# Output tiles in the spent v weights, and a new hand-written order, in a fused attention and GELU kernel

## The chip, the cores and the metric

The kernel runs on one core of one Trainium2 chip. The time is the device time of one execution in microseconds; the figure that is compared is the median over the runs. Before the change it is 206.4 us (three runs, 206.39 to 206.58). Beside the timed runs there is one profiled execution with a trace. Its own time is 207.25 us, and its span, from the first to the last instruction, is 205.3 us. Engines are named as the profile names them: PE (matmul), PEld (weight load), DVE (vector), ACT (scalar), POOL, and SP, which issues most of the DMAs.

## The reference

For x of 2048 rows by 640 columns in bf16, the result is x + A + B, where both branches start from one layer norm of x:

```python
xn = _layernorm(x, axis=-1)
return x + _A_ref(xn, A_wqkv, A_wo) + _B_ref(xn, B_w1, B_b1, B_w2, B_b2)
```

A is local attention with 32 heads of 20 columns. Every row attends to 8 rows, itself and those 2, 4, ... 14 rows back; rows before the start are masked. Queries, keys and values are xn @ wqkv, and the result goes through wo. B is a dense layer of 1536 columns with a bias and a tanh GELU, and a second dense layer with w2 and a bias.

## The kernel before

The rows are cut into 4 chunks of 512, each of 4 blocks of 128. Chunk n and block j or bl are the digits in the names of pieces below. Every piece is a short function that emits a few instructions, and the list ORDER (lines 42 to 74) gives the order in which all pieces are emitted. No scheduler moves anything afterwards: each engine runs its own instructions in the order of the list and waits, at an instruction, for the semaphores of what it needs. A piece that stands early in the list can therefore hold back everything behind it on its engine.

For one chunk the work is this.

- Statistics (`st` on DVE, or `su`, `ng`, `sq` on ACT for chunks 2 and 3), `rs` (square root on ACT, which loads a table), `rc` (reciprocal on DVE), and `xn`, the normalised rows (DVE in chunk 0, ACT after that).
- Transposes. Chunk 0 uses PE (`tp`) and copies out of PSUM (`tc`). Chunks 1 to 3 use one DMA transpose per block on SP's queue (also named `tc`, line 295). Chunk 1's stand at tc10 to tc13.
- Projections into q, k and v, transposed. In chunk 0 they are made in halves of 256 columns: `ga`, `gb`, `gd`, `ge` for q of the first pair of blocks, then `hj` followed by type (0 q, 1 k, 2 v), pair and column group, with the casts `hc` on ACT (line 398). Later chunks use `pj` (five 128x512 matmuls, line 339) and `pc` (a cast on ACT, line 403).
- Scores: eight `qk` products on DVE (line 436), then sums that fold five tiles into fewer, `pa` (line 471), in the buffer `half`. PE then adds the heads in `lg` (line 479) and ACT copies the logits (`cl`). The softmax follows on DVE and ACT (`mask`, `m`, `mx`, `ex`, `ss`, `ri`, `at`), and SP spreads the weights over partitions (`xd`, line 554).
- Values: eight `av` products on DVE (line 563), one sum `aa` that is an accumulating DMA on POOL's queue (line 573) in chunks 0 to 2 and a DVE instruction in chunk 3, then `ab` and `ot` on DVE. `half` is used again for the next chunk.
- The dense branch: `f1` (five matmuls, line 595) into PSUM and `ge` (GELU on ACT, line 611). The hidden tiles of chunk 3 lie in the spent q and k weights.
- The output: `o` followed by chunk, block and part 0 to 4. Parts 0 to 3 multiply hidden tiles with w2, part 4 multiplies `ot`'s result with wo (lines 631 and 633). `oc` copies the sum to a bf16 tile `osb` on ACT, and `od` adds it to the rows of the result by an accumulating DMA on POOL's queue. The last block goes another way (`oclo`, `ohi`, `ochi`, `ochd`).
- The result's rows are first written with x (`xp0`, `xp1`, `xp2`, on SP's queue) and then get the bias b2 (`xb`, on POOL's queue). `ldx`, `ld2` and `ldo` load the rest of x, then w2, then wo with b2.

Two pools matter for the order. `psA` has 6 PSUM buffers for nearly all results of PE but `o`; a matmul group waits until ACT has emptied an older buffer. `outp` has 2 tiles `osb`, so that an `oc` waits until the `od` before the last has landed.

The order before puts the weights' loads and the row copies among chunk 1's transposes on SP's queue: tc13, xp0, tc10, tc11, tc12, xp2, ldo, ld2.

Of the kernel before, what the change touches and what calls it, by code (L numbers as in the profile page):

```python
# [41 lines left out]
ORDER = """
wb st00a sum1 wa pad01 st00 rs00 ldx rc00 xn00a tp00a xn00b tp00b tc00a ga neg1 sq1 rs01 rc01 tc00b gb2 mean1 xn01
tp01 gb3 gb4 tc01a gd tc01b ho ge gc1 st03a st03 rs03 gc0 hj102 rc03 hc102 tb b1 hj101 hc101 st02a st02 rs02 hj100
hc100 xn03 tp03 tc03 pk hj202 rc02 xn02 tp02 tc02 gc4 hj201 hc201 hj111 st11a st10a hc111 st12a hj012 hc012 st11 hc202
st13a st13 hj112 hc112 st10 st12 rs1 qk010 rc1 qk000 qk011 hj110 f10_0 ge0_0 hj212 xn13 qk001 xn10 tc13 xn11 hc212
pa010 hj011 hj010 hc010 f10_11 f10_2 hc110 hc011 qk031 qk021 ge0_11 f10_10 xp0 qk020 pa000 su23 f10_6 xn12 ge0_10
qk030 pa020 su21 tc10 tc11 su22 hj200 hc200 f10_3 ge0_3 pa030 pa011 f10_9 tc12 su20 ng2 sq21 ge0_9 pa021 pj101 pc101
ge0_2 sq23 pj111 pj102 pj114 pc114 xp2 pc102 pj110 pc110 pj104 pa001 ge0_6 pa031 lg0 pc111 cl0 ldo xb3 xb2 pc104 mask
m0 mx0 ex0 pj112 pj103 pc103 pj113 pc113 ss0 ri0 pad11 pj100 pc100 pc112 qk121 qk120 hj211 sq20 hc211 qk101 ld2 pj124  # L50
qk100 sq22 pc124 f10_4 rs2 f11_6 pj121 rc2 ge0_4 pa120 qk110 f11_2 f10_1 ge0_1 pa121 qk111 xn21 pj123 pc123 ge1_6
pa122 pa100 pa110 xn23 f10_7 ge0_7 f11_8 tc23 f11_0 o000 xn20 tc20 tc21 ge1_2 f10_5 ge1_0 xb0 xn22 tc22 qk131 at0 xd00
ge1_8 f11_3 ge1_3 pa111 qk130 su32 pa101 pc121 f10_8 ge0_8 pad02 hj210 f11_5 pa130 pj120 pc120 pj200 pc200 pa112 pj211
pc211 pj210 pj212 pa131 pa102 pc210 hc210 pad12 pa132 lg1 av000 cl1 pj202 ge0_5 pj214 pc202 pj204 av001 aa00 m1 xd02
av021 pad21 av020 xd01 av011 av010 pj220 pj203 su33 ge1_5 su31 su30 ng3 sq33 xd03 av031 o001 pc212 pc203 o002 pc214
sq30 ab00 ot00 aa02 aa01 sq32 sq31 pj213 pc213 xp1 pj221 pj224 rs3 av030 ab02 pj122 pc122 pad22 rc3 ot02 o003 o004
oc00 od00 pj201 mx1 ex1 ss1 ri1 at1 xn31 pc220 xn30 f11_9 o020 o021 o022 o023 xd10 ab01 ot01 pc204 o024 oc02 pc201
aa03 tc30 ab03 f11_4 pc224 o030 o031 o032 pj223 o033 ot03 o034 xn33 av100 f12_3 av101 aa10 xn32 pc223 xd12 av120 xd13
f12_0 f11_11 av130 oc03 pc221 o010 o011 ge2_3 f12_11 o012 ge2_11 ge1_4 ge1_9 xd11 av110 av111 aa11 o013 o014 av121
pj222 pc222 av131 aa13 tc31 tc33 tc32 pj302 pj322 pj300 pc322 pj314 pc314 pj312 ab10 f11_1 ge1_11 ge1_1 f11_7 pj303  # L60
qk201 ot10 qk200 pa200 pc312 ge2_0 pj301 pc301 ab11 pa201 f11_10 pc302 ge1_10 qk211 ot11 od02 qk210 ab13 qk231 ot13
pj324 pc324 pj304 pc304 pa210 qk230 aa12 qk221 ab12 ge1_7 pj311 pa211 oc01 ot12 pa230 od01 f13_2 qk220 pc311 f12_8
pa212 od03 ge3_2 pa220 pc300 o130 pa231 pj313 pa221 o131 o132 o133 o134 oc13 pj310 f13_0 pc303 pc310 ge2_8 xb1 o120
pa202 pa232 pa222 lg2 o121 o122 pad31 pc313 qk300 f13_6 qk311 cl2 m2 qk310 f13_10 qk331 mx2 ge3_6 f13_8 qk330 ge3_0
f13_3 ge3_3 pa310 o123 qk301 o124 ex2 ss2 oc12 od12 f12_7 qk320 ri2 pa311 at2 xd23 pa330 pa300 qk321 f12_4 o110 o111
o112 pa301 o113 ge3_10 f12_10 pa320 pa312 o114 oc11 ge2_10 f12_6 f13_7 ge3_7 ge3_8 ge2_7 o100 o101 pa321 f12_2 xd21
od13 pa331 pa302 pa322 f12_5 o102 o103 ge2_6 ge2_5 o104 pa332 lg3 od11 oc10 od10 pj323 av210 pc323 av211 f12_9 cl3 m3
f13_1 xd22 xd20 ge3_1 pj321 av230 f12_1 ge2_1 aa21 av231 f13_5 ge3_5 av201 av200 aa23 f13_9 mx3 ge2_2 ge2_4 aa20 ab21
f13_4 ge2_9 ot21 ex3 ss3 ri3 ge3_4 f13_11 ge3_11 av220 ab23 o210 o211 at3 xd30 o212 o213 o214 ot23 oc21 od21 av221
aa22 pj320 o330 ab20 pc321 ot20 ge3_9 pad32 pc320 av300 o310 av301 o200 o201 o202 o203 o204 oc20 od20 o311 o230 o231  # L70
xd31 av310 o232 xd32 o233 o234 oc23 o312 o220 o221 o222 av311 aa31 ab22 ot22 o223 o224 od23 oc22 od22 av321 o313 av320
aa32 ab32 ot32 o320 o321 o322 o323 o324 oc32 od32 ab31 ot31 o314 oc31 od31 o300 xd33 o301 o302 o303 aa30 av331 ab30
ot30 o304 oc30 od30 av330 aa33 ab33 ot33 o331 o332 o333 o334 ohi xl oclo ochi ochd
""".split()


# [720 lines left out]
```

## Time and profile before

| what | value |
|---|---|
| median of 3 runs | 206.4 us |
| profiled execution: own time | 207.25 us |
| profiled execution: span | 205.3 us |
| PE busy | 200.1 us, 97% |
| DVE busy | 181.6 us, 88% |
| ACT busy | 127.1 us, 62% |
| POOL busy | 34.6 us, 17% |
| granted TensorE clock | 1.00 in every stretch |
| DMA moved | 31.77 MB, mean 155 GB/s |

The chain of waits that ended last goes through PE for 90% of the span. Busy times overlap between engines, and one matmul's row is longer than the distance to the next matmul on PE: the rows of 128x512 matmuls are 379 ns long, while five of them, started one behind the other, take 1.08 us. So this document counts PE's work by the distance between starts: 0.216 us for 512 columns, 0.109 us for 256 and 0.056 us for 128. ACT's and DVE's instructions overlap by some 0.1 us as well, and sums over a queue use distances between starts there too: 0.48 us for a cast of 512 columns, 0.27 us for 256, 0.58 us for a GELU, 0.81 us for an `xn`, 1.40 us for a `qk` or an `av`, 1.14 us for the first `pa` of a block and 0.60 us for its others.

### The profile page before, as it was taken

Reading aid. Unit: us, or ns where it says so; the run is one execution under the profiler, and the core shown is the slowest. Engines: PE = TensorE matmul, PEld = TensorE weight load, DVE = VectorE, ACT = ScalarE, POOL = GpSimd, SP = SyncE. Lnnn points to the kernel's source line nnn. Section 1 sums busy time; section 2 is a strip of 40 time slices with the busy share of each in tenths; the row PEclk is TensorE's granted clock in tenths of the full one; section 3 lists DMA queues with packets and bytes.
Section 4 is the critical chain, followed back from the end, with each engine's and each line's share of the span. In section 5 each row is a group of like instructions: output and inputs, shape, how many; then the busy total and the mean of one; then the engine's idle time right before and its main releaser. Section 6 shows DMA issues by size and latency. Waiting matters only on the chain.

```text
span 205.3 us, 3230 instructions
## 1 busy us (share of the span) xinstructions
PE 200.1 (97%) x1261; PEld 111.1 (54%) x1261; DVE 181.6 (88%) x226; ACT 127.1 (62%) x246; POOL 34.6 (17%) x49
## 2 busy tenths in 40 slices
PE   8899999999999999999999999999999999999994
PEld 3798655464454555554555555445544455555552
DVE  3489999389998999769999999899998999699992
ACT  6388998999966998856425735564535794111210
POOL 2000000440000242202260060003104223111120
PEclk9999999999999999999999999999999999999999
DMA  6999599899259299989999067005462997972253
GB/s 209 390 395 374 185 140 323 303 258 199 58 100 252 86 173 190 156 128 182 189 188 191 8 73 122 0 0 68 103 134 32 164 190 118 209 116 28 28 66 64
DMA packets 27335, 31.77 MB, mean 155 GB/s; under 512 B 9272, under 2 KB 22072, under 8 KB 27320
## 3 DMA queue, kind: packets, MB, share of 16 engines
q0 software_dynamic: 7408, 12.78, 39.0%
q1 hardware_dynamic: 19600, 18.58, 32.8%
q8 instruction: 10, 0.16, 0.3%
q10 hardware_dynamic: 312, 0.20, 0.3%
q14 instruction: 5, 0.04, 0.1%
HBM read 10.00 MB, written 7.54 MB: 85 GB/s over the span
## 4 chain that ended last, share of the span: by engine, by line
PE 90%; DMA 4%; ACT 3%; issue 1%; SPq 0%; DVE 0%
PE lo L631 29%; PE pps L339 24%; PE hps L595 22%; PE hi L633 7%; PE gps L383 5%; DMA wq_sb<-in_A_wqkv_dram 3%; DMA xnT<-xn 2%; ACT xn L266 2%; PE gps L352 1%; PE L L479 1%; ACT qT L398 1%; PE tp L283 0%; ACT trash L224 0%; ACT hT L611 0%; SPq L131 0%
## 5 line engine op out<-in xcount | busy, mean ns | idle before, releaser
L595 PE MATMUL hps<-xnT,w_sb 128*128 128x512 bf16 x240 | 55.6, 379 | 0.0
L436 DVE TENSOR_TENSOR half<-qT,kT 128x2560 bf16<-128x2560 bf16 x32 | 46.7, 1484 | 1.0 <-PE L L479 0.9
L631 PE MATMUL lo<-w_sb,hT 128*128 128x512 bf16 x144 | 41.3, 379 | 0.0
L595 PEld LDWEIGHTS <-w_sb 128*128 128x128 bf16 x240 | 23.1, 98 | 26.2
L471 DVE TENSOR_TENSOR half<-half 128x1024 bf16<-128x1024 bf16 (+1 forms) x44 | 36.5, 881 | 0.0
L638 ACT CAST osb<-lo 128x512 bf16<-128x512 f32 x15 | 8.8, 584 | 37.1 <-PE hi L633 18.3
L633 PE MATMUL hi<-w_sb,hT 128*128 128x128 bf16 x144 | 31.5, 219 | 0.0
L611 ACT ACTIVATE hT<-hps,b1T 128x512 bf16<-128x512 f32 x36 | 24.0, 692 | 6.5 <-PE hps L595 5.6
L563 DVE TENSOR_TENSOR half<-vT,x_sb 128x2560 bf16<-128x2560 bf16 x16 | 23.0, 1487 | 3.3 <-DMA x_sb<-e 3.2
L644 POOL DMA_DIRECT2D out_dram<-osb x15 | 13.7, 959 | 72.2 <-ACT osb L639 72.2
L573 POOL DMA_DIRECT2D half<-half x12 | 15.6, 1302 | 56.0 <-DVE half L563 56.0
L563 DVE TENSOR_TENSOR half<-vT,ax 128x2560 bf16<-128x2560 bf16 x16 | 23.0, 1482 | 1.2 <-PE L L479 1.2
L631 PEld LDWEIGHTS <-hT 128*128 128x128 bf16 x144 | 14.1, 98 | 17.2 <-issue 0.4
L631 PE MATMUL lo<-wo,oT 128*128 128x512 bf16 x80 | 23.1, 379 | 0.0
L339 PE MATMUL pps<-xnT,wq_sb 128*128 128x512 bf16 x75 | 18.5, 380 | 0.4 <-DMA xnT<-xn 0.4
L339 PE MATMUL pps<-xnT,wv_sb 128*128 128x512 bf16 x75 | 18.3, 379 | 0.0
L339 PE MATMUL pps<-xnT,wk_sb 128*128 128x512 bf16 x75 | 18.0, 379 | 0.0
L633 PE MATMUL hi<-wo,oT 128*128 128x128 bf16 x80 | 16.9, 219 | 0.0
L176 ACT ACT_TABLE_LOAD x12 | 15.4, 1283 | 0.9 <-PEq L781 0.7
L633 PEld LDWEIGHTS <-hT 128*128 128x128 bf16 x144 | 14.1, 98 | 1.9
L582 DVE TENSOR_TENSOR half<-half 128x1280 bf16<-128x1280 bf16 x16 | 13.1, 821 | 0.5 <-DMA half<-half 0.4
L403 ACT CAST vT<-pps 128x512 bf16<-128x512 f32 x15 | 8.8, 587 | 6.9 <-PE pps L339 6.9
(91 smaller groups left out, 262.3 us busy)
## 6 DMA issues: line engine op xcount, KB each, us to landing
half<-half POOLq DMA_DIRECT2D x12, 640.0 KB, 6.9
w_sb<-in_B_w_dram SPq DMA_DIRECT2D x4, 960.0 KB, 11.3
out_dram<-osb POOLq DMA_DIRECT2D x15, 160.0 KB, 3.5
ax<-e SPq DMA_DIRECT2D x8, 256.0 KB, 4.7
x_sb<-e SPq DMA_DIRECT2D x8, 256.0 KB, 4.9
out_dram<-b2bc POOLq DMA_DIRECT2D x3, 640.0 KB, 9.6
x_sb<-in_A_x_dram SPq DMA_DIRECT2D x1, 1280.0 KB, 12.9
out_dram<-x_sb SPq DMA_DIRECT2D x2, 640.0 KB, 4.7
```

Source lines behind the costliest of these rows:

```text
L176: nc.scalar.activation(warm[:], nc.const_aps.tensor(0.0, [P, 1], F32), func)
L339: nc.tensor.matmul(ps[:], lhsT=wqkv_p[which][:, ti, to, :], rhs=xnT[:, ti, :], start=(ti == 0), stop=(ti == KT - 1),)
L436: nc.vector.tensor_tensor(out=half[:, j, h], in0=q[:, :, at].unsqueeze(1).to_broadcast([P, W // 2, KT, P]), in1=window(k, h, at), op=ALU.mult,
L471: nc.vector.tensor_tensor(out=kept, in0=kept, in1=gone, op=ALU.add)
L563: nc.vector.tensor_tensor(out=half[:, j, h], in0=window(qkv_tile(n, 2), h, cs), in1=ax_view(n)[:, j, ws, :].unsqueeze(2).to_broadcast([P, ...
L573: nc.gpsimd.dma_start(a, b, accum_op=ALU.add, max_dma_last_dim=CUT)
L582: nc.vector.tensor_tensor(out=a, in0=a, in1=b, op=ALU.add)
L595: nc.tensor.matmul(ps[:], lhsT=w1_sb[:, ti, ft * P : (ft + 1) * P], rhs=tiles["xnT", n][:, ti, :], start=(ti == 0), stop=(ti == KT - 1),)
L611: nc.scalar.activation(hT, tiles["hps", n, ft][:], ACT.Gelu_apprx_tanh, bias=b1T[:, ft : ft + 1], scale=1.0)
L631: nc.tensor.matmul(lo[:], lhsT=lhs, rhs=rhs[:, 0:CH], start=first, stop=last)
L633: nc.tensor.matmul(hi[:, 0 : D - CH], lhsT=lhs, rhs=rhs[:, CH:D], start=first, stop=last)
L644: nc.gpsimd.dma_start(rows, tiles["osb", n, bl][:], accum_op=ALU.add)
```

## The change

The tiles `osb` of chunk 3 and of block 0 of chunk 2 no longer come from the pool `outp`. They lie in the weights of v, which hold five slots of 128x640:

```diff
+    def out_tile(n, bl):
+        if (n, bl) == (2, 0) or n == NCH - 1:
+            return wqkv[2][:, bl if n == NCH - 1 else BPC, :]
+        return outp.tile([P, D], BF16, tag="osb", name="osb")
+
     def do_oc(n, bl):
-        osb = outp.tile([P, D], BF16, tag="osb", name="osb")
+        osb = out_tile(n, bl)
 ...
     def do_oclo():
-        osb = outp.tile([P, D], BF16, tag="osb", name="osb")
+        osb = out_tile(*last)
```

The list ORDER is new throughout; it holds the same pieces. Its part up to chunk 1's `lg`:

```diff
-wb st00a sum1 wa pad01 st00 rs00 ldx rc00 xn00a tp00a xn00b tp00b tc00a ga neg1 sq1 rs01 rc01 tc00b gb2 mean1 xn01
-tp01 gb3 gb4 tc01a gd tc01b ho ge gc1 st03a st03 rs03 gc0 hj102 rc03 hc102 tb b1 hj101 hc101 st02a st02 rs02 hj100
-hc100 xn03 tp03 tc03 pk hj202 rc02 xn02 tp02 tc02 gc4 hj201 hc201 hj111 st11a st10a hc111 st12a hj012 hc012 st11 hc202
-st13a st13 hj112 hc112 st10 st12 rs1 qk010 rc1 qk000 qk011 hj110 f10_0 ge0_0 hj212 xn13 qk001 xn10 tc13 xn11 hc212
-pa010 hj011 hj010 hc010 f10_11 f10_2 hc110 hc011 qk031 qk021 ge0_11 f10_10 xp0 qk020 pa000 su23 f10_6 xn12 ge0_10
-qk030 pa020 su21 tc10 tc11 su22 hj200 hc200 f10_3 ge0_3 pa030 pa011 f10_9 tc12 su20 ng2 sq21 ge0_9 pa021 pj101 pc101
-ge0_2 sq23 pj111 pj102 pj114 pc114 xp2 pc102 pj110 pc110 pj104 pa001 ge0_6 pa031 lg0 pc111 cl0 ldo xb3 xb2 pc104 mask
-m0 mx0 ex0 pj112 pj103 pc103 pj113 pc113 ss0 ri0 pad11 pj100 pc100 pc112 qk121 qk120 hj211 sq20 hc211 qk101 ld2 pj124
 ...
+ho sum1 pad02 st00a tb st00 wb rs00 neg1 sq1 rc00 xn00a tp00a xn00b tp00b ldx mean1 tc00a rs01 rc01 pad01 xn01 tp01
+tc01a tc00b tc01b b1 st03a ga gb2 gb3 gb4 gd ge gc1 hj101 st03 rs03 gc4 st02a st02 gc0 rc03 xn03 rs02 rc02 hj100 tp03
+tc03 xn02 tp02 tc02 st11a st11 hj201 hc100 hj102 hc102 hc101 hj212 hc212 hj011 hc011 hc201 hj112 hc112 st10a st10
+st13a st13 st12a st12 wa rs1 f10_0 ge0_0 qk011 hj111 hc111 rc1 xn12 tc12 qk001 xn10 tc10 hj012 qk000 qk010 hj010 xn11
+hj110 hc110 pa000 hc012 pk hc010 qk020 qk021 su22 qk030 qk031 tc11 xn13 tc13 ld2 f10_3 pa020 pa001 ldo xp0 xb0 f10_9
+hj200 ge0_9 hj202 hc202 pa021 f10_11 ge0_11 pa010 f10_8 su21 su20 su23 ng2 f10_2 ge0_3 hc200 sq20 ge0_2 xp2 pj102
+pc102 pj110 sq21 pc110 pj101 pc101 ge0_8 pa030 pa011 pj111 pj100 pc100 pj112 pa031 pc111 lg0 cl0 pj104 xb2 pc112 mask
+m0 mx0 ex0 ss0 pad11 pj113 pj103 pc103 ri0 pc104 pj114 pc114 pc113 qk130 qk100 qk131 qk121 pj123 pc123 sq23 f11_5 sq22
 ...
```

On SP's queue chunk 1's transposes now come first, in the order tc12, tc10, tc11, tc13, and behind them stand ld2, ldo, xp0 and xp2. The end of the list:

```diff
-aa22 pj320 o330 ab20 pc321 ot20 ge3_9 pad32 pc320 av300 o310 av301 o200 o201 o202 o203 o204 oc20 od20 o311 o230 o231
-xd31 av310 o232 xd32 o233 o234 oc23 o312 o220 o221 o222 av311 aa31 ab22 ot22 o223 o224 od23 oc22 od22 av321 o313 av320
-aa32 ab32 ot32 o320 o321 o322 o323 o324 oc32 od32 ab31 ot31 o314 oc31 od31 o300 xd33 o301 o302 o303 aa30 av331 ab30
-ot30 o304 oc30 od30 av330 aa33 ab33 ot33 o331 o332 o333 o334 ohi xl oclo ochi ochd
+ot20 f13_11 pad32 pc321 av311 av310 xd33 o310 o330 xd32 o200 o201 o202 o203 o204 ge3_8 oc20 ot23 o311 aa31 ab31 o230
+o231 xb3 av330 o232 o233 o234 oc23 av331 o312 ab22 ot22 o220 o221 o222 o223 o224 av320 ge3_11 o313 av321 aa32 ab32
+ot32 ot31 oc22 od22 o320 o321 o322 o323 xd30 o324 av300 av301 aa30 ab30 ot30 oc32 o314 oc31 od31 od23 o300 o301 o302
+aa33 od20 o303 o304 oc30 od32 ab33 od30 o331 o332 ot33 o333 o334 xl oclo ohi ochi ochd
```

The stores od31, od23, od20 and od32 now stand together near the end of POOL's queue, and xb3, which stood with xb2, stands behind od21. Every engine has the same matmuls, vector operations, activations, table loads and DMAs as before, in another order.

More of the change, by code (lines that the diff above doesn't have):

```diff
@@ L48 @@
-qk030 pa020 su21 tc10 tc11 su22 hj200 hc200 f10_3 ge0_3 pa030 pa011 f10_9 tc12 su20 ng2 sq21 ge0_9 pa021 pj101 pc101
-ge0_2 sq23 pj111 pj102 pj114 pc114 xp2 pc102 pj110 pc110 pj104 pa001 ge0_6 pa031 lg0 pc111 cl0 ldo xb3 xb2 pc104 mask
-m0 mx0 ex0 pj112 pj103 pc103 pj113 pc113 ss0 ri0 pad11 pj100 pc100 pc112 qk121 qk120 hj211 sq20 hc211 qk101 ld2 pj124
-qk100 sq22 pc124 f10_4 rs2 f11_6 pj121 rc2 ge0_4 pa120 qk110 f11_2 f10_1 ge0_1 pa121 qk111 xn21 pj123 pc123 ge1_6
-pa122 pa100 pa110 xn23 f10_7 ge0_7 f11_8 tc23 f11_0 o000 xn20 tc20 tc21 ge1_2 f10_5 ge1_0 xb0 xn22 tc22 qk131 at0 xd00
@@ L53 @@
[L53 to L67, printed above, removed]
@@ L68 @@
-f13_1 xd22 xd20 ge3_1 pj321 av230 f12_1 ge2_1 aa21 av231 f13_5 ge3_5 av201 av200 aa23 f13_9 mx3 ge2_2 ge2_4 aa20 ab21
-f13_4 ge2_9 ot21 ex3 ss3 ri3 ge3_4 f13_11 ge3_11 av220 ab23 o210 o211 at3 xd30 o212 o213 o214 ot23 oc21 od21 av221
-aa22 pj320 o330 ab20 pc321 ot20 ge3_9 pad32 pc320 av300 o310 av301 o200 o201 o202 o203 o204 oc20 od20 o311 o230 o231
-xd31 av310 o232 xd32 o233 o234 oc23 o312 o220 o221 o222 av311 aa31 ab22 ot22 o223 o224 od23 oc22 od22 av321 o313 av320
-aa32 ab32 ot32 o320 o321 o322 o323 o324 oc32 od32 ab31 ot31 o314 oc31 od31 o300 xd33 o301 o302 o303 aa30 av331 ab30
@@ new lines @@
+hj110 hc110 pa000 hc012 pk hc010 qk020 qk021 su22 qk030 qk031 tc11 xn13 tc13 ld2 f10_3 pa020 pa001 ldo xp0 xb0 f10_9
+hj200 ge0_9 hj202 hc202 pa021 f10_11 ge0_11 pa010 f10_8 su21 su20 su23 ng2 f10_2 ge0_3 hc200 sq20 ge0_2 xp2 pj102
+pc102 pj110 sq21 pc110 pj101 pc101 ge0_8 pa030 pa011 pj111 pj100 pc100 pj112 pa031 pc111 lg0 cl0 pj104 xb2 pc112 mask
+m0 mx0 ex0 ss0 pad11 pj113 pj103 pc103 ri0 pc104 pj114 pc114 pc113 qk130 qk100 qk131 qk121 pj123 pc123 sq23 f11_5 sq22
+rs2 rc2 f10_5 hj211 hc211 qk120 qk101 pa130 f10_4 ge0_4 xn22 tc22 ge0_5 qk111 hj210 hc210 pj121 xn20 at0 pa120 pj124
@@ new lines @@
+pc124 f11_2 xn23 f11_0 qk110 f11_8 ge1_8 tc23 f11_3 pa100 tc20 ge1_5 f10_7 ge0_7 pa121 xn21 f10_1 ge0_1 f10_10 ge1_3
+pa101 pa110 pc121 o000 ge1_0 f10_6 ge0_6 f11_6 pj120 pa102 pc120 su30 tc21 ge1_6 pj213 pj202 pc202 pad12 pa131 pa111
+pa122 xd00 pa112 pj211 pa132 lg1 ge0_10 o001 pj210 pc213 pc211 xd03 av001 pj200 pc200 cl1 pc210 ge1_2 av000 pj201
+pc201 xd02 av020 pj220 aa00 av021 aa02 m1 mx1 pj214 pc214 av030 av031 pj203 su31 su32 su33 xd01 ab00 pj122 ot00 ng3
+sq30 av010 f11_10 xp1 av011 pc122 ab02 ex1 ot02 o002 ss1 ri1 f11_4 aa03 ab03 pj212 pc212 o003 o004 oc00 od00 sq33
@@ new lines @@
+pc203 ot03 sq31 sq32 rs3 f12_11 at1 xd10 pj224 pc224 pad21 xd13 pad22 xd12 aa01 xd11 o020 o021 o022 o023 o024 oc02 rc3
+xn32 xn31 tc31 tc32 ab01 ot01 pj222 pc222 o030 o031 o032 xn30 tc30 pc220 o033 o034 oc03 pj204 pc204 o010 o011 av101
+av100 av120 aa10 av131 av110 av111 aa11 av121 f11_11 ge1_11 av130 aa13 xn33 tc33 f12_0 ge1_4 f11_1 ge1_1 qk201 ge2_0
+o012 o013 o014 f11_7 f13_2 ge1_7 pj223 pc223 ab10 ot10 qk200 pa200 f11_9 ge1_9 f12_3 ge2_3 od03 ge2_11 ab11 qk211
+pj324 pc324 pj313 pc313 pj302 ot11 qk210 ab13 pj310 pc310 oc01 ot13 qk230 aa12 f12_7 qk231 pj311 pc311 pj314 pc314
@@ new lines @@
+ab12 ge2_7 pj303 pc303 o130 pa230 o131 pj312 o132 ge1_10 pa210 pa201 pc312 f13_10 pa231 od02 ot12 pad31 pj301 qk221
+o133 qk220 o134 oc13 pa211 pa212 pj300 pc302 pc300 pc301 o120 pj304 ge3_2 pc304 o121 f13_4 pa220 ge3_10 pa202 pa221
+ge3_4 pa232 pa222 lg2 cl2 qk300 m2 mx2 qk330 qk331 qk301 o122 qk311 ex2 ss2 ri2 qk310 o123 f12_8 ge2_8 pa300 f12_2 at2
+xd20 xd22 f12_5 pa301 pa330 xd23 pa310 f12_4 f13_3 ge3_3 od01 ge2_4 xd21 o124 oc12 xb1 od12 f12_6 pa331 o110 pa311
+od13 o111 o112 o113 f13_6 ge3_6 qk320 o114 oc11 f13_9 o100 o101 qk321 o102 pa320 ge2_2 ge3_9 pa312 f13_7 ge3_7 ge2_5
@@ new lines @@
+pj322 pc322 f12_1 ge2_1 pj221 pc221 o103 o104 oc10 pa321 od11 pa302 pa322 pa332 lg3 av210 av211 pj320 pc320 pj323
+f13_0 ge3_0 f12_10 ge2_10 av230 av231 od10 cl3 ge2_6 av200 m3 f12_9 mx3 ex3 ge2_9 av201 f13_1 ge3_1 o210 aa21 ab21
+f13_8 ot21 ss3 av221 aa23 ri3 aa20 at3 xd31 pj321 f13_5 ge3_5 av220 aa22 o211 o212 ab23 o213 o214 pc323 ab20 oc21 od21
+ot20 f13_11 pad32 pc321 av311 av310 xd33 o310 o330 xd32 o200 o201 o202 o203 o204 ge3_8 oc20 ot23 o311 aa31 ab31 o230
+o231 xb3 av330 o232 o233 o234 oc23 av331 o312 ab22 ot22 o220 o221 o222 o223 o224 av320 ge3_11 o313 av321 aa32 ab32
```

## The prediction

> **What bounds the kernel now.** I read the page's busy times first, then the engines in 40 slices, then PE's waits.
>
> ```profile
> span 205.3 us, 3230 instructions
> PE 200.1 (97%) x1261; PEld 111.1 (54%) x1261; DVE 181.6 (88%) x226; ACT 127.1 (62%) x246; POOL 34.6 (17%) x49
> ...
> PE   8899999999999999999999999999999999999994
> ```
>
> PE is full in every slice but the first two and the last. Its waits, longest first:
>
> ```profile
> PE gps L352 <- DMA wq_sb<-in_A_wqkv_dram: 1.0, 1, 1.0
> PE idle L449 <- PEq L781: 0.8, 1, 0.8
> PE pps L339 <- DMA xnT<-xn: 0.4, 1, 0.4
> PE tp L283 <- DVE xn L268: 0.2, 1, 0.2
> ```
>
> From `ga` at 6.77 on, PE waits once: for chunk 1's last transpose, at 29.5 (0.4 here, 0.59 by the distance between starts). From 30.28 to the last matmul, which ends at 202.52, it is never idle. The change removes no matmul, so no more is to be had than 0.59, part of the 1.0 at the opening, and the tail. What can be lost has no such limit: whatever PE waits for in the new order is added to the end. So the question is which results come later than PE asks for them.
>
> The timeline from 11 to 40 us, of DVE, and then the lines of all engines around `lg0`:
>
> ```profile
> 12.31 0.40 DVE L268 TENSOR_SCALAR xn<-x_sb,mv,rstd 128x640 bf16<-128x640 bf16 x1
> ...
> 12.96 0.45 DVE L268 TENSOR_SCALAR xn<-x_sb,mv,rstd 128x640 bf16<-128x640 bf16 x1
> 13.40 1.67 DVE L212 BATCH_NORM_STATS2 stats<-x_sb 128x6 f32<-128x320 bf16 x4
> ...
> 17.43 1.44 DVE L436 TENSOR_TENSOR half<-qT,kT 128x2560 bf16<-128x2560 bf16 x1
> ...
> 31.21 4.76 DVE L471 TENSOR_TENSOR half<-half 128x2048 bf16<-128x2048 bf16 x6
> 38.63 0.21 DVE L496 TENSOR_TENSOR Lb<-Lb,mask 32x128 bf16<-32x128 bf16 x1 [2.66 <-ACT Lb L492]
> ```
>
> ```profile
> 36.86 1.05 PE L479 MATMUL L<-half,head_of 128*32 128x512 bf16 x16
> ...
> 37.52 1.07 ACT L492 CAST Lb<-L 128x512 bf16<-128x512 f32 x2
> ```
>
> DVE has no idle time from 13.40, when x's blocks 4 to 7 have landed (13.38 in the trace), to 35.97, when the last `pa` of chunk 0 ends. PE takes that up in `lg0` at 36.86. The slack is 0.89 us. At chunk 1 the same hand-over has 0.11 (last `pa` ends 65.67, `lg1` 65.78), at chunk 2 0.42 (127.99 and 128.41), at chunk 3 0.09 (153.88 and 153.97). PE and DVE are both full, and bind each other at the four `lg`.
>
> **The change, step by step.**
>
> *The list ahead of `lg0`* decides, I think. Counting PE's pieces there in both lists, the new one lacks f10_6, f10_10, pj104 and pj114 and has f10_8, pj100 and pj112: one group of five 0.216 matmuls fewer, 1.08 us. So from `lg0` on PE has 165.66 us left before (36.86 to 202.52) and 166.74 after. PE gets to `lg0` sooner; DVE does not. Ahead of it stand the same eight `qk`, eight `pa` and the statistics of blocks 4 to 7, and these cannot start before 13.40. Without any wait of its own DVE ends at 35.97 again.
>
> *DVE does have a wait of its own.* The new list puts qk020, which needs the q of the second pair, behind four `qk`, `rc1` and one `pa`: 17.43 + 4 x 1.40 + 0.28 + 1.14 = 24.45. The last cast of that q, hc010, stands deep in ACT's queue. I follow ACT from the opening.
>
> - PE's opening: in the new list xn03 and xn02 are asked for by tp03 and tp02 right behind hj101 and hj100; hj102 and hj202, which filled PE there, are behind them. DVE can start on blocks 2 and 3 at 9.63 (landed 9.61) as before; st02a then follows at 10.78, where before it stood behind a wait of 0.36 for rs03 and began at 11.27. st02 ends at 11.90, and rc03 (0.19), xn03 (ends 12.48), rc02 (0.19) and xn02 (ends 13.12) follow. PE, dense from `ga` at 7.0 (tp01 now fills the wait for wq, tb waits for b1's last packet, 5.10), is through with hj100 at 7.0 + 50 x 0.056 + 20 x 0.109 = 12.0. It waits 0.5, then 0.4 for tp02, and starts hj201 at 13.45.
> - hj011 then ends at about 16.9 (hj201, hj102, hj212 and itself, 30 x 0.109, and 0.2 for the last row). ACT's hc011 starts there. From its end, 17.39, ACT is dense: hc201 0.48, hc112 0.27, rs1 with the table load that GELU needs 1.61, ge0_0 0.58, hc111 0.48, three `xn` 2.44, hc110 0.48, hc012 0.27, pk 0.16, hc010 0.58. That is 7.35; hc010 ends at 24.74, seen by DVE at 24.80.
>
> So DVE waits 0.35, its last `pa` ends at 36.32, and `lg0` runs at 36.38. PE, 22.33 us of work behind hj201, would be there at 35.78; it waits 0.6. The end: 36.38 + 166.74 = 203.12, against 202.52: **0.6 us later**. The opening's 0.9 costs nothing by itself: it is spent inside that wait. If that cover were gone, it would cost 0.9 less the 0.59. The 0.59 in front of the first `pps` goes, and is worth nothing either: what is late next is `lg0`.
>
> *The transposes of chunk 1.* xn13 ends on ACT at 24.74 + 0.79 (su22) + 0.92 = 26.45; its transpose is the last. Two rows price it. In before's chunk 1 the last one was issued at 26.56 and landed at 30.15, 3.6 us; in chunk 2, with nothing else on SP's queue, the last was issued at 57.64 and landed at 60.05, 2.4 us. I take 2.4, as the new queue has nothing ahead of it: 28.9, and pj102 is due at 13.45 + 15.85 = 29.3. By 3.6 PE waits 0.75 and comes to `lg0` at 36.5, 0.15 more on the sum. The Trainium skill (DMA: Bandwidth & Descriptors, section Issuing engines are not separate DMA queues) says that all DMAs share the same 16 engines and interleave; by that, transposes without xp0 beside them give the 2.4, though the 3.6 was for one issued after xp0 had landed (26.06), so the rule alone does not explain the row.
>
> *The loads behind them.* ld2, ldo, xp0 and xp2 took from 28.99 to 43.63 before, the last landing being w2's; from 28.9 on they take to about 43.5. w2 is first asked for by o000, at 58: nothing. xb0 and xb2 are late with b2, but the next on POOL's queue, aa00, came at 69.57: nothing.
>
> *`lg1`.* DVE's chain hangs on `lg0`: 0.48 earlier than before (36.38 for 36.86), `mask` to `qk` as before, the same 21.5 us of `qk`, `pa`, `rc2` and `at0`: last `pa` at 65.19. PE, again 1.08 of work ahead, is there at 36.38 + 28.89 = 65.27. No wait, with 0.1 to spare. If DVE were as late as before (65.67), `lg1` would run at 65.73 with 137.83 of PE's work left, and the end be 203.56, 1.0 later instead of 0.6.
>
> *Behind that* the lists agree better: at `lg2` PE has 0.26 more left than before and at `lg3` the same, with the same DVE work ahead. at3 stands 0.85 us (one `ab`) sooner behind `lg3`, so chunk 3's `xd` starts at 170.8 rather than 171.3, and the 1.8 us for which DVE waited there (ot20 ends 174.34, av300 starts 176.14) takes up the delay. By the same sums each last `ot` comes 0.7 us or more ahead of its part 4.
>
> *The output tiles.* ACT is idle 37.1 us ahead of its copies to `osb`, all behind PE; no wait for a landed store is seen. Worth nothing. At the end four stores stand together on POOL: od31 can start at about 195.7, the others 0.7 apart, od30 at 200.3. A store was 3.5 us from issue to landing: 203.8, ahead of the last store of ACT, at 205.0 by before's 204.39. Nothing, with 1 us of cover.
>
> **The sum**: +0.6 us on the profiled execution (207.25 to 207.85), and on the median, 0.85 below it, **207.0 us**. A measurement of this kernel can tell about 0.2%, 0.41 us, from no change.
>
> **The rivals.**
>
> 1. *DVE does not wait for hc010* (not slower than the measurement can tell). ACT's sum from 17.39 is of measured distances, but its start rests on the opening. If ACT is 0.35 sooner, `lg0` runs at 36.05 and the end is 0.27 later: 206.67. DVE's floor, 13.40 and 22.5 us of work, forbids less.
> 2. *ACT holds up PE through PSUM.* ACT is busy 10.9 of 11 us from 20 to 31 before. By the same sums pj101 is due at 31.5 and the buffer that it needs is freed by ge0_3 at 31.2; f11_0 is due at 51.5, ge0_5 frees at 50.9; f10_10 at 56.9, freed at 56.6. From 0.3 us of lateness on, ACT costs PE what it is late; 1 us too little in my sum of ACT's queue gives 0.7 more: 207.7.
> 3. *Nothing waits* (faster). If x's blocks land 1.2 us sooner than 9.61 and 13.38, DVE is ahead of PE throughout. PE's 194.6 us of work from `ga` at 7.0 then end at 201.6, 0.9 sooner than before: 205.5. Nothing in the new list moves those loads on SP's queue.
> 4. *The last stores queue up.* If the four do not overlap, 195.7 + 5 x 3.5 = 213 ends behind everything. Against it: before, stores issued at 193.59 and 194.95 landed at 196.92 and 198.55, 3.3 and 3.6 after their own issue.
>
> **Chances**: forecast 0.42, rival 1 0.24, rival 2 0.22, rival 3 0.07, rival 4 0.05. Rivals 2 and 4 are slower by over 0.2%, as is the forecast: slower 0.69, same 0.24, faster 0.07. The range leaves out rivals 3 and 4 and the worst of 2: 206.4 to 208.3.
>
> **What would show it.** Right: in the changed kernel's trace PE waits in front of tp03 and tp02, no longer in front of the first `pps`; DVE waits for ACT's cast of q in front of a `qk` near 24.5; PE waits for `pa` in front of `lg0` near 36.4, and hardly at all after that. Wrong: waits of PE for ACT's casts or GELUs (rival 2), an `lg0` that PE reaches after DVE, or a last store on POOL's queue that lands behind ACT's.

## The result and the profile after

| | before | after |
|---|---|---|
| median of the same measurement, 10 runs each | 206.59 us | 208.25 us |
| lowest | 206.39 | 207.18 |
| ratio after to before | 1 | 1.0063, 95% interval 1.0035 to 1.009 |
| profiled execution, own time | 207.25 | 209.1 |
| its span | 205.3 | 207.3 |

The changed kernel is slower by 0.6%, about 1.3 us, as the ratio has it. Two of its ten runs (211.04 and 214.66) fell under a lower granted clock (0.992); such runs count in the medians, here and below, but not in the ratios. A second measurement of the same kernel, the first experiment below, gave 207.77 against 206.69 and a ratio of 1.0059 [1.0027, 1.0091].

The page of the kernel after, the same parts as were shown of before, and its chain by engine:

```profile
span 207.3 us, 3202 instructions
...
PE 200.0 (96%) x1239; PEld 111.9 (54%) x1261; DVE 182.2 (88%) x226; ACT 127.6 (62%) x246; POOL 34.6 (17%) x49
...
PE   8899999999999999999889999999999999999994
...
PE 84%; DVE 6%; ACT 4%; DMA 3%; issue 1%
```

PE's busy time is the same 200 us. (The 22 matmuls fewer are records missing from the trace; the 1261 weight loads are all there.) The chain that ended last now runs through DVE for 6%, where PE had 90% of it before, and two slices in the middle of PE's row have dropped to 8. PE's waits of the kernel after name both places:

```profile
PE hps L595 <- DMA xnT<-xn: 1.5, 1, 1.5
PE idle L449 <- PEq L786: 0.8, 1, 0.8
PE tp L283 <- DVE xn L268: 0.6, 1, 0.6
PE L L479 <- DVE half L471: 0.2, 1, 0.2
...
```

The wait for wq and the one ahead of the first `pps` are gone. In their place stand one of 0.6 in the opening, where tp01 waits for the `xn` of chunk 0's block 1, a small one at `lg0` (L479), and one of 1.5 that no step of the prediction had: an `hps` that waits for a DMA transpose.

DVE's timeline of the kernel after from 23 to 37 us, then the lines around `lg0`, shows the predicted hand-over:

```profile
22.81 1.21 DVE L471 TENSOR_TENSOR half<-half 128x2048 bf16<-128x2048 bf16 x1
24.53 5.70 DVE L436 TENSOR_TENSOR half<-qT,kT 128x2560 bf16<-128x2560 bf16 x4 [0.50 <-ACT qT L398]
30.14 5.90 DVE L471 TENSOR_TENSOR half<-half 128x2048 bf16<-128x2048 bf16 x7
```

```profile
35.47 0.41 PE L479 MATMUL L<-half,head_of 128*32 128x512 bf16 x3
...
36.09 1.02 PE L479 MATMUL L<-half,head_of 128*32 128x512 bf16 x13 [0.21 <-DVE half L471]
```

DVE stands idle for 0.50 ahead of qk020, until ACT's cast hc010 (line 398) ends at 24.50. From there it runs without a gap to the end of its last `pa` at 36.04, and `lg0`, which PE had begun at 35.47, goes on at 36.09. Before, `lg0` ran at 36.86, so this hand-over came 0.76 sooner than in the profile of before. From it to the end PE had 165.69 us left before, up to DVE's last addition (202.55), and now takes 168.34 (to 204.43). Of the 2.65 more, 1.08 is the group that the new list has moved behind `lg0`; the rest, 1.57, is all but covered by the `hps` at 104 us (1.47 in the view, 1.63 by the distance between starts):

```profile
101.56 1.24 PE L595 MATMUL hps<-xnT,w_sb 128*128 128x512 bf16 x5
104.27 1.24 PE L595 MATMUL hps<-xnT,w_sb 128*128 128x512 bf16 x5 [1.47 <-DMA xnT<-xn]
```

That is f13_2, the first piece to read chunk 3's transposed rows. Its turn was at 102.6, and the last transpose of that chunk landed at 104.13.

### The profile page after: what moved, and what is told of

The parts are those of the page before. It is cut to its first block, busy times and chain, and to the rows that moved or that the text cites. A ratio compares the mean times of both kernels' runs of the same rounds, so it can differ in the third digit from the quotient of the medians.

```text
span 207.3 us, 3202 instructions
## 1 busy us (share of the span) xinstructions
PE 200.0 (96%) x1239; PEld 111.9 (54%) x1261; DVE 182.2 (88%) x226; ACT 127.6 (62%) x246; POOL 34.6 (17%) x49
## 4 chain that ended last, share of the span: by engine, by line
PE 84%; DVE 6%; ACT 4%; DMA 3%; issue 1%
PE lo L631 26%; PE hps L595 20%; PE pps L339 20%; PE hi L633 8%; PE gps L383 4%; DMA xnT<-xn 3%; DVE half L471 3%; DVE half L436 3%; PE idle L449 2%; ACT xn L266 2%; PE gps L352 1%; PE L L479 1%; PE tp L283 1%; ACT qT L398 1%; ACT L176 1%
## 5 line engine op out<-in xcount | busy, mean ns | idle before, releaser
L436 DVE TENSOR_TENSOR half<-qT,kT 128x2560 bf16<-128x2560 bf16 x32 | 46.2, 1481 | 3.5 <-DMA half<-half 2.3
L631 PE MATMUL lo<-w_sb,hT 128*128 128x512 bf16 x137 | 39.9, 379 | 0.0
L471 DVE TENSOR_TENSOR half<-half 128x1024 bf16<-128x1024 bf16 (+1 forms) x44 | 36.0, 879 | 0.1
L649 POOL DMA_DIRECT2D out_dram<-osb x11 | 12.3, 1164 | 62.9 <-ACT osb L644 62.9
L631 PE MATMUL lo<-wo,oT 128*128 128x512 bf16 x75 | 22.2, 379 | 0.1
L339 PE MATMUL pps<-xnT,wk_sb 128*128 128x512 bf16 x75 | 18.5, 379 | 0.0
L643 ACT CAST osb<-lo 128x512 bf16<-128x512 f32 x11 | 6.5, 587 | 19.0 <-PE lo L631 14.2
L308 POOL DMA_DIRECT2D out_dram<-b2bc x4 | 6.5, 1626 | 39.9 <-DMA out_dram<-x_sb 39.9
```

What stands on the lines that cost most here:

```text
L339: nc.tensor.matmul(ps[:], lhsT=wqkv_p[which][:, ti, to, :], rhs=xnT[:, ti, :], start=(ti == 0), stop=(ti == KT - 1),)
L436: nc.vector.tensor_tensor(out=half[:, j, h], in0=q[:, :, at].unsqueeze(1).to_broadcast([P, W // 2, KT, P]), in1=window(k, h, at), op=ALU.mult,
L471: nc.vector.tensor_tensor(out=kept, in0=kept, in1=gone, op=ALU.add)
L631: nc.tensor.matmul(lo[:], lhsT=lhs, rhs=rhs[:, 0:CH], start=first, stop=last)
L649: nc.gpsimd.dma_start(rows, tiles["osb", n, bl][:], accum_op=ALU.add)
```

## The experiments

**Theories.** T, from this profile: two hand-overs cost the time, hc010 ahead of `lg0` in every execution and f13_2 as well. R: no single wait, but many small ones of PE for ACT's buffers. All ratios are to the kernel before, run beside the kernel in question; "last addition" is the start of DVE's last add (line 661, or 666 after the change).

**The changed kernel again, and each hand-over mended.** Four kernels, run side by side on one chip: the changed kernel, f13_2 moved, xn11 moved, both.

```diff
-o012 o013 o014 f11_7 f13_2 ge1_7 pj223 pc223 ab10 ot10 qk200 pa200 f11_9 ge1_9 f12_3 ge2_3
+o012 o013 o014 f11_7 ge1_7 pj223 pc223 ab10 ot10 qk200 pa200 f11_9 ge1_9 f12_3 f13_2 ge2_3
...
-hj010 xn11 hj110 hc110 pa000 hc012 pk hc010 qk020 qk021
+hj010 hj110 hc110 pa000 hc012 pk hc010 xn11 qk020 qk021
```

> The changed kernel itself, for a second profile and as the yardstick of this chip. Theory T (two late hand-overs: lg0, where DVE's wait for the cast hc010 costs PE 0.3 to 0.6 us, and f13_2, where PE waits for the last transpose of chunk 3, a wait that differs from run to run): 0.7 to 2.0 us slower than before, the profile shows PE waiting 0 to 2 us for the DMA xnT at f13_2, and the span less that wait is within 0.4 of 205.7. Rival R (many small waits for ACT's casts and PSUM buffers): the same time, but the wait at f13_2 of the first profile (1.6 us) is a single event, under 0.3 here, with the time lost elsewhere.

> Only f13_2 moved, from behind f11_7 to behind f12_3, so that the first use of chunk 3's transposes on PE comes 3.2 us later. T: PE's wait for DMA xnT falls below 0.3 us, the time is 0.6 to 1.4 us below the changed kernel's of this job, about 207.0, and its spread is smaller. R: within 0.3 us of the changed kernel.

> Only xn11 moved, from ahead of hj110 to behind hc010, so that ACT's casts of the second pair's q come 0.8 us sooner. T: DVE's wait near 24 us goes, lg0 runs 0.4 to 0.5 us sooner, and the time is 0.3 to 0.5 us below the changed kernel's. R (PE late at lg0 for itself): lg0 and the time are unchanged within 0.2 us.

> Both moves, f13_2 behind f12_3 and xn11 behind hc010. T: both gains add up, 1.0 to 1.8 us below the changed kernel, which is 206.3 to 206.8, level with before. R: at most 0.4 us below the changed kernel.

| kernel | median (before: 206.69) | ratio [95%] | wait at f13_2 |
|---|---|---|---|
| e0_again | 207.77 | 1.0059 [1.0027, 1.0091] | none |
| e1_f13_later | 207.77 | 1.0047 [1.0021, 1.0073] | none |
| e2_xn11_behind | 207.65 | 1.0048 [1.0012, 1.0084] | none |
| e3_both | 207.39 | 1.0022 [0.9989, 1.0054] | none |

T's second half is not borne out as a cause of the usual time. In e0_again, the same kernel, the last transpose landed at 101.42 and f13_2 ran at 102.37 without a wait, and moving f13_2 left the median where it was. The wait of the first profile is an event of some executions: 209.1 less its 1.63 is the 207.5 of e0_again's own profile.

T's first half holds by the traces; by the times it is not told apart, as the intervals of the four ratios overlap. In e2_xn11_behind the cast came 0.43 sooner (24.02), but x's blocks 4 to 7 landed at 13.44, so that the last `pa` ended at 35.97, as in e0_again; the median is 0.12 lower, where T had 0.3 to 0.5. In e3_both the cast comes early and DVE's gap is gone, as its timeline shows:

```profile
22.75 1.22 DVE L471 TENSOR_TENSOR half<-half 128x2048 bf16<-128x2048 bf16 x1
23.89 5.69 DVE L436 TENSOR_TENSOR half<-qT,kT 128x2560 bf16<-128x2560 bf16 x4
29.50 5.90 DVE L471 TENSOR_TENSOR half<-half 128x2048 bf16<-128x2048 bf16 x7
```

The last `pa` ends at 35.39 in place of 35.99. R's many waits have no support: none of the four profiles has a wait of PE for ACT. But e3_both gained only 0.4 on the median, R's number and not the 1.0 to 1.8 of T. Of the 0.60 won at `lg0`, 0.2 is given back at `lg1`, which now runs as DVE's last `pa` of chunk 1 ends (64.50 for both; 0.14 apart in e0_again). And the last addition, 0.41 sooner than in e0_again, did not shorten the span: 205.6 in both. Something behind the last addition had taken over.

**Behind the last addition.** The page does not count POOL's DRAIN, an instruction at the end of the program, as busy; the view of that line shows it (columns: shortest, median and longest in ns, then first and last start). Of the kernel before, after, and e3_both:

```profile
L792 POOLq DRAIN  x3: 40/102/4651, 199.5 to 205.0; - x3
```

```profile
L797 POOLq DRAIN  x3: 40/93/5146, 201.4 to 207.1; - x3
```

```profile
L797 POOLq DRAIN  x3: 40/93/5497, 199.3 to 205.3; - x3
```

The longest of the three is the first one. It begins when od30 is issued and ends 1.31 or 1.32 us after od30 has landed, in every trace of this study. SP waits for the landings of SP's and ACT's stores, and the kernel ends about 0.75 after the later of the two engines.

| trace | POOL's last store lands | POOL's DRAIN ends | SP is through | span |
|---|---|---|---|---|
| before | 202.88 | 204.19 | 204.54 | 205.3 |
| after | 205.25 | 206.57 | 206.39 | 207.3 |
| e0_again | 203.50 | 204.81 | 204.71 | 205.6 |
| e3_both | 203.52 | 204.83 | 204.31 | 205.6 |
| f1_stores_early | 202.88 | 204.20 | 204.48 | 205.2 |

So in the new order it is POOL that ends the kernel, by 0.1 to 0.5, because od23, od20, od32 and od30 stand together there. Three of them were issued earlier in the next kernel, which keeps both moves of e3_both.

```diff
-o230 o231 xb3 av330 o232 o233 o234 oc23 av331
+o230 o231 xb3 od20 av330 o232 o233 o234 oc23 od23 av331
...
-oc32 o314 oc31 od31 od23 o300 o301 o302 aa33 od20 o303 o304 oc30 od32 ab33 od30
+oc32 od32 o314 oc31 od31 o300 o301 o302 aa33 o303 o304 oc30 ab33 od30
```

> The changed kernel with f13_2 behind f12_3, xn11 behind hc010 (as in e3_both) and, new, the stores od23, od20 and od32 each as soon as its tile is copied, so that od30 stands alone at the end. Theory T: in the new order POOL's last DRAIN ends the kernel; in every profile it ends 1.31 after POOL's last store lands (203.52 and 204.83 in e3_both), behind SP's (204.31 there). With od30 alone it lands 0.4 or more sooner, DRAIN ends by 204.4, the span is 0.4 to 0.5 shorter (205.1), the median 206.9 to 207.0. Rival: the last stores of SP and ACT decide as in the kernel before, and the stores on POOL's queue are worth nothing: 207.4 as e3_both.

Measured: 207.13 (before 206.78), ratio 1.002 [0.9997, 1.0043]. The stores' lines between 190 and 206 us, of e3_both and then of f1_stores_early (count, size, us from issue to landing):

```profile
out_dram<-wv_sb POOLq DMA_DIRECT2D x4, 160.0 KB, 5.1
```

```profile
out_dram<-wv_sb POOLq DMA_DIRECT2D x3, 160.0 KB, 3.3
```

Alone, od30 lands 3.3 after its issue, POOL's DRAIN is through before SP, and from the last addition to the end of the span it takes 2.7 us in place of 3.3. By the trace the 0.5 is shown; by the times, 0.70 over before in e3_both and 0.35 here, it fits (T had 206.9 to 207.0) but the intervals overlap.

**The kernel before once more, and two parts of the change alone**, in before's own order.

> The kernel before, profiled a second time, because its first profile (span 205.3) lies above most of its runs. Theory T: that profile had late loads (wq landed at 6.73, x blocks 4 to 7 at 13.38); in most runs they land about 0.5 sooner, as in the profiles of the changed kernel (5.9 and 12.9), the whole chain behind them is 0.5 sooner, and the span is 204.7 to 204.8. Then the changed kernel loses about 0.85 to a usual run of the kernel before. Rival: the loads land as in the first profile, the difference arises later, and the span is 205.3 again.

It gave 206.78 against 206.78, and its profile was a late one again: wq at 6.72, x blocks 4 to 7 at 13.36, span 205.2. The early loads that T looked for came with the next kernel, which differs from before only in the output tiles.

```diff
 def do_oc(n, bl):
-    osb = outp.tile([P, D], BF16, tag="osb", name="osb")
+    osb = out_tile(n, bl)
```

> One part alone: the kernel before in its own order, with only the output tiles of chunk 3 and of chunk 2's block 0 in the spent weights of v. Theory T: worth nothing, 206.6 to 206.8 and a ratio within 0.1% of 1. Rival: the tiles free ACT's copies or hold something (a store that must wait for readers of the weights), and the time moves by 0.2 us or more.

Median 207.12 against 206.78, ratio 0.9997 [0.9975, 1.0018]: no difference that can be told. Its profiled execution (206.28, span 204.5, the fastest of its twelve) had wq at 6.02 and x blocks 4 to 7 at 12.71, each about 0.7 sooner than in the profile of before, and everything behind them is sooner by the same: `ga` 6.06 for 6.77, `lg0` 36.16 for 36.86, last addition 201.80 for 202.55. In these profiles the old order moves with its loads, one for one.

The other part alone, the loads of w2, wo and b2 and the row copy xp0 behind chunk 1's transposes (xp2 stands there already):

```diff
-ge0_11 f10_10 xp0 qk020 pa000
+ge0_11 f10_10 qk020 pa000
...
-f10_9 tc12 su20
+f10_9 tc12 ld2 ldo xp0 su20
...
-cl0 ldo xb3 xb2
+cl0 xb3 xb2
...
-qk101 ld2 pj124
+qk101 pj124
```

> One part alone: the kernel before in its own order, with only ld2, ldo and xp0 moved behind chunk 1's last transpose (tc12), so that SP issues the four transposes first. Theory T: the wait of PE for the last transpose (0.59 by starts) goes, and since PE is behind DVE at lg0 by 0.89 there, all of it is won: 0.4 to 0.6 less, about 206.2. That would be the worth of this part without the new list. Rival: the gain is lost again at lg1, where DVE's last pa was only 0.11 ahead of PE, and the time is as before, 206.6.

Median 207.23 against 206.78, ratio 1.0018 [0.9995, 1.0042], so the theory's 206.2 falls. Its profiled execution (208.08) is the slowest of the twelve, and what follows is read from that one. The 0.59 ahead of the first `pps` is indeed won: `lg0` runs 22.37 behind hj201 in place of 22.92. It is lost again before `lg1`, as the rival had it, but not at the hand-over that the rival named (last `pa` 65.19, `lg1` 66.30). ACT's waits from 20 to 62 us, PE's from 8 to 62, and the DMAs from 43 to 60, all of e5_loads_behind:

```profile
ACT xn L266 <- DMA xnT<-xn: 2.5, 1, 2.5
```

```profile
PE hps L595 <- ACT hT L611: 0.8, 1, 0.8
```

```profile
out_dram<-b2bc POOLq DMA_DIRECT2D x2, 640.0 KB, 10.1
out_dram<-b2bc POOLq DMA_DIRECT2D x1, 480.0 KB, 5.8
xnT<-xn SPq DMA_TRANSPOSE x4, 3.7
```

and of e4_tiles_alone, in the same window, the transposes:

```profile
xnT<-xn SPq DMA_TRANSPOSE x4, 2.4
```

The second row copy lands late (43.4 in place of 34.0), POOL's three `xb`, which accumulate onto those rows, start at 44.0 in place of 37.9, and now run until 57.5, beside chunk 2's transposes. The first of these takes 4.9 us (53.18 to 58.11). ACT waits 2.5 for the `xn` buffer that it holds, the GELUs behind that `xn` are late, and PE stops for 0.99 (0.8 in the view) in front of an `hps` that is due at 58.7. The Trainium skill (DMA: Bandwidth & Descriptors, section Issuing engines are not separate DMA queues) says that DMAs started by the scalar, sync or gpsimd engine run on the same 16 DMA engines and interleave. The trace fits that: the transposes stand on SP's queue and the `xb` on POOL's, and the first transpose takes 4.9 us beside them and 2.4 without.

**Is it the collision? Two kernels that should take it away.** One keeps the loads behind the transposes and puts xb3 near the end, behind od20 (the new list has it there too, behind od21). The other leaves the loads where they were and moves only xp0 behind the transposes.

```diff
-pj104 pa001 ge0_6 pa031 lg0 pc111 cl0 xb3 xb2
+pj104 pa001 ge0_6 pa031 lg0 pc111 cl0 xb2
...
-oc20 od20 o311
+oc20 od20 xb3 o311
```

> e5_loads_behind with xb3 moved behind od20, near the end, where the new order has it. Theory T: in e5_loads_behind the three xb (POOL's accumulating DMAs, 44.0 to 57.5) ran beside chunk 2's transposes, the first of which took 4.9 in place of 2.4; ACT waited 2.5 for its xn buffer and PE 0.99 in front of an hps. Without xb3 there the xb end by 53.5, the transposes take 2.4, that gap is gone, and the time is 206.2 to 206.3. Rival: the gap comes from w2 and wo themselves, standing ahead of the row copies: the time stays at 207.2.

```diff
-ge0_11 f10_10 xp0 qk020 pa000
+ge0_11 f10_10 qk020 pa000
...
-f10_9 tc12 su20
+f10_9 tc12 xp0 su20
```

> The kernel before with one DMA moved: xp0, the row copy of blocks 0 to 3, behind chunk 1's last transpose; the loads of w2, wo and b2 stay where they were. Theory T: the last transpose lands by 29.1, PE's wait of 0.59 in front of the first pps goes as in e5_loads_behind, and since both row copies still land by 35 or so, POOL's xb start at 38 as before and are through before chunk 2's transposes: nothing is given back, 206.2, about 0.5 less than the kernel before. Rival: the saved time is lost at lg1 or by a later collision as in e5_loads_behind: 206.7 to 207.2.

g4_loads_xb3: 207.05 against 206.96, ratio 0.9995 [0.9961, 1.003], with half of the runs at 206.0 to 206.9 and half at 207.2 to 209.1. The mechanism goes T's way, if not all of it: the two `xb` left end at 55.2 (53.5 expected), the first transpose takes 3.35 (2.4 expected), ACT's wait is 0.9, PE has no wait at all from 8 to 62 us, and the profiled execution has a last addition at 201.54, the earliest of all. The rival falls in this trace: w2 and wo stand where e5_loads_behind has them, and the gap is gone. The time that T gave from this is undercut by that execution (206.04, the fastest of its twelve) and not met by the median. Against the slowest execution of e5_loads_behind, the comparison shows what the collision does to an execution, not what it costs in the median; why the runs scatter so is open.

g3_xp0_behind: **206.09 against 206.96, ratio 0.9959 [0.9936, 0.9983]**, the fastest kernel of this study, ahead of both before and after. All that PE waits for in its profile:

```profile
PE gps L352 <- DMA wq_sb<-in_A_wqkv_dram: 1.1, 1, 1.1
PE idle L449 <- PEq L781: 0.8, 1, 0.8
```

The wait for the last transpose is gone and none has come in its place. The `xb` run from 39.8 to 53.5, just ahead of chunk 2's transposes, which take 2.4. That profile had the latest loads of all (wq at 7.46, 0.73 later than in before), and yet its last addition came at 202.64, 0.09 behind before's. Counted from the landing of x's blocks 4 to 7 (14.10) it comes after 188.54 us, in before after 189.17: the 0.6 of the wait is kept to the end.

**The opening of the new order.** In its profiles `ga` starts at 7.2 to 7.35 though wq has landed at 5.8 to 6.5, since tp01 stands ahead of it and waits 0.6 to 0.8 for the `xn` of block 1 (in e0_again tb waits for b1 as well, 0.7).

```diff
-ho sum1 pad02 st00a tb st00
+ho sum1 pad02 st00a st00
...
-tc00a rs01 rc01 pad01 xn01 tp01 tc01a tc00b tc01b b1 st03a ga gb2 gb3
+tc00a ga rs01 rc01 tc00b gb2 pad01 xn01 tp01 tc01a tc01b st03a gb3
...
-gc4 st02a st02 gc0 rc03 xn03 rs02 rc02 hj100 tp03
+gc4 tb b1 st02a st02 gc0 hc101 rc03 xn03 rs02 rc02 hj100 hj102 hj202 tp03
...
-hj201 hc100 hj102 hc102 hc101 hj212
+hj201 hc100 hc102 hj212
...
-ge0_9 hj202 hc202
+ge0_9 hc202
```

> The changed kernel with the opening in the old manner: ga and gb2 ahead of tp01 again, tb and b1 behind gc4 and hc101 behind gc0, and hj102 and hj202 ahead of tp03 as work for PE while xn03 and xn02 are made. Theory T: in the changed kernel ga waits for tp01 (7.2 to 7.35 in all its profiles, though wq landed at 5.8 to 6.2), and hc010 comes at 24.4 however early the loads land, while the kernel before starts ga as wq lands and shifts with it. Here ga starts at about 6.1, hc010 ends 0.5 or more sooner (before 23.9), DVE runs without a gap from the landing of x blocks 4 to 7, lg0 is released 22.6 after that (35.4 for 12.8, in place of 36.07), and the median is 207.2 to 207.3. Rival: the opening is covered, as the prediction said (the waits at tp03 and tp02 are spent inside the wait at lg0): 207.8.

208.69 against 206.96, ratio 1.0078 [1.0045, 1.0112]: slower than the changed kernel, and T's number falls. `ga` did start at 6.28, but the two groups put ahead of tp03, 1.09 of work, filled a gap that is hardly there (0.13 ahead of tp02 in the kernel after): tp03 came at 12.80, hj201 then waited 0.5 for ACT's copy tc02, and hc010 ended at 24.98, 0.53 later than in e0_again. DVE's timeline:

```profile
25.02 5.70 DVE L436 TENSOR_TENSOR half<-qT,kT 128x2560 bf16<-128x2560 bf16 x4 [0.67 <-ACT qT L398]
```

So the run does not say what the opening alone is worth. It does say once more what hc010 is worth: 0.53 later there, the last addition is 0.54 later (203.29). The median is further off, 0.92 above e0_again's on another chip, and the trace does not show why. The last kernel joins this opening to the moves of f1_stores_early.

> The opening of g1_opening, with f13_2 and xn11 moved as in e3_both and the three stores early as in f1_stores_early. Theory T: with the opening mended DVE is already at its floor, so xn11 adds nothing; the stores take POOL's DRAIN out of the end. lg1 stays with DVE at 22.6 + 29.1 behind the landing, and PE has 1.1 more left there than the kernel before, so the new order still loses about 0.3: 206.9 to 207.0. Rival: the gains add up, 0.5 for the opening, 0.4 for xn11 and 0.4 for the stores, and the time is 206.5, ahead of the kernel before.

207.3 against 206.96, ratio 1.0021 [0.9995, 1.0047], where T had 206.9 to 207.0, and no better than f1_stores_early without the opening. The last addition comes at 202.42; in e4_tiles_alone, the old order with loads about as early, it comes at 201.80.

## Why the prediction was right, and where its size was off

**Direction and mechanism.** Over all eight profiles of the new order one rule, fitted to them, gives the end of chunk 0's last `pa` within 0.05: the later of hc010's end plus 11.54 and the landing of x blocks 4 to 7 plus 22.53. The prediction had the same two: hc010 at 24.80 with 11.5 of work behind it, and 13.40 with 22.5.

| trace | x blocks 4 to 7 land | hc010 ends | by the rule | last `pa` ends | last addition |
|---|---|---|---|---|---|
| after | 12.91 | 24.50 | 36.04 | 36.04 | 204.43 |
| e0_again | 12.52 | 24.45 | 35.99 | 35.99 | 202.75 |
| e1_f13_later | 12.84 | 24.34 | 35.88 | 35.89 | 202.66 |
| e2_xn11_behind | 13.44 | 24.02 | 35.97 | 35.97 | 202.99 |
| e3_both | 12.85 | 23.52 | 35.38 | 35.39 | 202.34 |
| f1_stores_early | 13.19 | 23.69 | 35.72 | 35.74 | 202.51 |
| g1_opening | 12.89 | 24.98 | 36.52 | 36.53 | 203.29 |
| g2_all | 12.59 | 23.84 | 35.38 | 35.43 | 202.42 |

Where hc010 decides (e0_again, e1_f13_later, g1_opening) the last addition follows 166.8 after that, which is the predicted 0.06 and 166.74. The wait at qk020 was 0.50 for 0.35, `lg0` 36.1 for 36.38, PE's wait there 0.55 by starts for 0.6. No profile of the changed list shows rival 2, PE held up by ACT's casts or GELUs.

**Right as well.** The transposes of chunk 1: the last took 2.4 (26.06 to 28.45, 28.9 forecast) and `pps` did not wait. `lg1` had nothing to spare: the last `pa` ends 0.13 ahead of it in the kernel after, 0.14 in e0_again. The output tiles alone made no difference that can be told. (The page's row was read too strongly: of ACT's 37.1 us ahead of those copies the view by forms puts 27.1 behind PE, and 9.4 behind nothing that it shows.)

**The opening went another way.** Its sign, waits of 0.5 and 0.4 ahead of tp03 and tp02, is not in the trace. PE's rows of the kernel after, from 4.8 to 14.5 us:

```profile
7.12 0.45 PE L283 MATMUL tp<-ident,xn 128*128 128x128 bf16 x5 [0.62 <-DVE xn L268]
...
10.20 2.35 PE L383 MATMUL gps<-xnT,wk_sb 128*128 128x256 bf16 x20
12.38 0.87 PE L283 MATMUL tp<-ident,xn 128*128 128x128 bf16 x10
```

PE waits at tp01, and the first matmul of `ga` starts at 7.41 (its weight load at 7.35), not at 7.0. PE is through with hj100 at 12.38, not 12.0, when xn03 has long been ready (11.88, for 12.48), and tp02 waits 0.13. The two errors partly cancel: hj201 starts at 13.09 for 13.45. ACT's queue from hc011's start to hc010's end took 7.93 for 7.83, so that sum was right, and hc010 came 0.24 sooner than forecast because of the opening.

**The mis-sized term** is the first of the two in the sum. The prediction set a `lg0` 0.48 sooner against 1.08 us more work behind it. The second term measures 1.06 (166.70 from the release of `lg0` in e0_again against 165.64 in e4_tiles_alone). The first depends on the loads. In the old order `lg0` moves with them, from 36.86 in the profile of before to 36.16 in e4_tiles_alone; in the new one it hangs on hc010 and stays at 36.05 with the earliest loads (12.52) and 36.10 with later ones (12.91); with late ones, at 13.4, this list was not profiled. Against the late profile the gain is 0.8, against the early one 0.1, and the loss is about 0.3 or 0.95. The prediction made its sum on one profile, which was a late one, and carried the difference over to the median. That most runs of before have earlier loads is inferred: no landing of a timed run is on record, and both profiles of before were late ones, with spans of 205.3 and 205.2; but most of its runs have spans of 204.4 to 205.1. Rival 3 asked what early loads would do and got the sign wrong: it gave them to the new kernel alone, while the old one gains from them too.

**The step that failed** is the last one of the output tiles' paragraph, "Nothing, with 1 us of cover". The stores did overlap (od30 landed 3.8 after its issue, so rival 4 was wrong too), but the end is not a landing: POOL's DRAIN comes 1.3 after it. The cover was -0.1 to -0.2, and -0.5 once `lg0` was mended.

**Luck.** The forecast was 0.6 us and the ratio says 1.3. The median of 208.25 lies inside the stated range by 0.05 us, and the range went up to 208.3 to take in most of rival 2, which did not happen.

**What it did not look at.** "The lists agree better" behind `lg1` passed over f13_2, which asks for chunk 3's transposes 0.64 us sooner than pj302 did (102.6 for 103.24). They run beside an accumulating DMA of POOL (aa10), and the slowest of them took 9.8 us in the profile after, 7.1 in e0_again and 7.0 in before, where chunk 2's take 2.4 to 3.1. The margin behind the last landing was 1.04 in before and 0.95 in e0_again, so the new list is hardly tighter there; why the landing came 2.7 later in the profile after is open. And the moved loads were followed only along POOL's queue ("the next on POOL's queue, aa00, came at 69.57: nothing"). In the new list nothing came of it, since xb3 is taken out of that stretch; in the old list the same move cost one execution 1.0 us ahead of `lg1`, while the `xb` and the transposes of another queue were in flight together. The median of that kernel is 0.45 above before's (207.23 for 206.78), and the interval of its ratio takes in 1.

**Still open.** Lowest against lowest run, the two measurements of the change give 0.8 and 0.9 us. At loads between the early and the late profile the two terms and the DRAIN give 0.4 to 1.1 us, and the ratios say 1.2 to 1.3 with intervals from 0.6 to 1.9. About half of the changed kernel's runs lie 0.4 us or more above its lowest, and of those only the first profile is a trace. How much of the difference is executions with a wait at f13_2 was not settled: e1_f13_later, without it, has the same median.

## What to carry to other kernels

A sum made on one profiled execution must be made again for a profile with other landings: ask of each order what it hangs on, and whether it moves with the loads. When a DMA is moved, look past its own queue at what will be in flight beside it, and past the DMA to what accumulates on its bytes. At the end of a kernel, count the issuing engine's last instruction and not the last landing.

## What the runs showed of the hardware that was not expected

- POOL's DRAIN at the end of the program ends 1.31 to 1.32 us after the last store of POOL's queue has landed, in all traces; for SP's and ACT's stores SP is through 0.15 after the landing.
- A DMA transpose of one 128x640 block takes 2.4 us from issue to landing with no accumulating DMA beside it (chunk 2 of e4_tiles_alone), 3.35 and 4.9 beside accumulating DMAs of 640 KB (`xb`), and up to 9.8 beside one of 640 KB between SBUF tiles (aa10).
- Four accumulating stores of 160 KB issued 0.54 apart land 0.8 or more apart: in e3_both the second to fourth of the queue took 5.7, 6.0 and 6.3, where one alone takes 3.3 to 3.4 (f1_stores_early; 3.3 to 3.6 for the last five of before).
- The first loads, which all twelve kernels issue in the same order (wq's at 1.20 to 1.21 us), land up to 1.7 us apart from one profile to the next (wq at 5.78 to 7.46), with the clock at 0.998 or more. Two profiles of one program are 0.01 (before) and 0.36 (after) apart.
